# Order of two small VectorE steps in a fused attention and MLP kernel: mixing product of the outputs ahead of phi of q

**Chip, cores, metric.** One Trainium2 chip, one of its cores. The metric is the device time of one execution in microseconds (us), lower is better. Executions of a kernel agree within about 0.3%, apart from a slow state of the chip that is left aside.

## The reference, cut to what matters

The kernel computes x + A(norm(x)) + B(norm(x)). B is a token-mixing MLP. A is an attention of 32 heads over 2048 tokens in 4 segments, with softmax inside a segment and a memory M, z of the segments before. The change touches only A:

```python
phi = lambda t: jnp.where(t > 0, t + 1.0, jnp.exp(t))
for s in range(N):                                   # 4 segments of 512 tokens
    p = softmax(einsum('bhqd,bhkd->bhqk', qs, ks) * scale + mask)
    a_dot = einsum('bhqk,bhkd->bhqd', p, vs)
    pq = phi(qs)
    a_mem = einsum('bhld,bhde->bhle', pq, M) / (einsum('bhld,bhd->bhl', pq, z)[..., None] + 1e-06)
    outs.append(g * a_mem + (1.0 - g) * a_dot)       # the mixing
    M = M + einsum('bhld,bhle->bhde', phi(ks), vs); z = z + phi(ks).sum(...)
return o @ wo
```

## The kernel before

After the MLP (up to about 388 us of the span) attention runs in 32 units: unit `u` is one group of four heads in segment `u // 8`. In the iteration of unit `u` TensorE computes the logits of `u`, the outputs of `u - 1` (`weigh`, three parts), and between them dense work in matmuls of 512 columns: the projections q, k, v of later units and the output products with `wo`. ScalarE takes the exponentials, GpSimd applies the causal mask, VectorE does the rest in small steps. The steps wait in a queue, `side`; TensorE's dense work stops at fixed places, and at each stop one step is issued:

```python
N_GRP = 8; N_UNIT = 32

def dense(self, n, side=True):                      # ... cut
    stop = min(at + n, 8)
    if self.side and side:
        stop = min([stop] + [x for x in stops if x > at])
    with fw.group(reads=reads(), writes=[self.R_bank[b]]):
        for i in range(at, stop):
            mm(b, i)
    # ...
    if stop == 8:
        end(b)                                       # copy out of PSUM: qT, kT, vA or fin
        self.jobs.popleft()
    elif self.side and stop in stops:
        self.side.popleft()()                        # one small step

# attention(), iteration of unit u, after the three parts of weigh(u - 1):
if u:
    self.weigh(u - 1, 2)
    steps = self.combine(u - 1)                      # [scales, products, add]
    last = steps[-1]
    steps[-1] = lambda u=u, last=last: (last(), self.o_transpose_dma(u - 1))
    self.side.append(steps.pop(0))                   # scales
if N_GRP <= u:
    self.side.append(lambda u=u: self.phi_q(u))
if u:
    self.side.extend(steps)                          # products, add + transposing transfer
if u + 1 < N_UNIT:
    self.side.append(lambda u=u: (self.phi_k(u + 1), self.k_transpose(u + 1)))
```

The steps themselves, with the tile names that the profile shows:

```python
def phi(self, dst, R_dst, src, R_src, k, u):         # two VectorE instructions
    # ...
    mt[:] = min(et[:], 1.0)                          # "mtmp<-etmp"
    dst = max(src + 1.0, mt[:])                      # "pqT<-qT,mtmp" for q

def combine(self, u):                                # ... cut
    # scales:   two small instructions, "srec<-ost", "srec<-srec,gate"
    # products: 1024 elements a partition, "prod<-ost,srec" (srec broadcast over 32)
    # add:      512 elements a partition, "o_s<-prod"

# logits(): after the exponential of ScalarE, one GpSimd instruction a block
for v, kb, _ in blocks:
    d = self.pT[:, v % 2, :, PT_OFF[kb]:PT_OFF[kb] + P]
    fw.op("pool", lambda e: e.affine_select(d, d, pattern=[[0, 4], [1, P]], compare_op=ALU.is_ge,
                                            fill=0.0, base=0, channel_multiplier=-1), ...)

# weigh(u, part): one group of matmuls; the whole group waits for what any of it reads
reads = list(R_vA)
if s:
    reads += [self.R_pqT[k], self.R_MZbf[g]]         # phi of q of this unit, the memory
reads += [R[pb][kb] for kb in range(last + 1) for R in (self.R_pu, self.R_pd)]
```

So phi of q of unit `u` must be done when `weigh(u, 0)` begins, early in the next iteration.

## Time and profile before

| | |
|---|---|
| time, median (fast runs) | 652.8 us (652.59 to 652.9) |
| span of the profiled run | 651.1 us |
| TensorE busy | 645.8 us (99%) |
| VectorE busy | 428.1 us (66%), in 800 instructions |
| GpSimd busy | 153.9 us (24%); 128 masks take 105.3 of it |
| attention, from the first logits | 387.8 us to the end |

The names in the profile: PE is TensorE's matmuls, PEld its weight loads (they run ahead of the matmuls), DVE is VectorE, POOL is GpSimd, ACT is ScalarE, SPq the queue that issues transfers. A row of the timeline has start, duration, engine, line, operation, out<-in, shapes and count; in brackets the idle time of the engine ahead of it and what ended it. Nearly all matmuls stand under L199, a helper, so one goes by tiles. The rows themselves are in the prediction.

### The profile page before, as it was taken

The numbers are of one execution on the slowest core, as the hardware profiler recorded it, in microseconds if no ns is written. First come the engines' busy times: TensorE is split into PE (matmuls) and PEld (weight loads), VectorE is DVE, ScalarE is ACT, GpSimd is POOL, SyncE is SP. The second block draws the span as 40 slices with busy tenths as digits, with TensorE's granted clock in tenths as the row PEclk, the third lists the DMA queues.
The fourth block names the chain that finished last, engine by engine and source line by source line (L and its number), as shares of the span: only waits on it lengthen the run. The fifth ranks groups of instructions, "written<-read, shape, count | busy, mean of one in ns | idle before, by whom it ended". The sixth has DMA issues, their size and how long they took to land.

```text
span 651.1 us, 11170 instructions
## 1 busy us (share of the span) xinstructions
PE 645.8 (99%) x4611; PEld 303.2 (47%) x4611; DVE 428.1 (66%) x800; ACT 281.4 (43%) x305; POOL 153.9 (24%) x179
## 2 busy tenths in 40 slices
PE   8999999999999999999999999999999999999998
PEld 3444444444444444444444444444544444445544
DVE  6975675665556664744738325766787877777896
ACT  7543232232210000110101047778767778888770
POOL 2500000000011220220202203343334444554440
DMA  9804233242498967538262946988544456445325
GB/s 306 212 0 130 65 106 89 64 116 79 129 257 206 270 205 209 156 103 229 80 208 98 267 126 174 179 169 197 120 116 96 125 147 109 126 98 128 106 93 139
DMA packets 181963, 95.00 MB, mean 146 GB/s; under 512 B 100248, under 2 KB 167832, under 8 KB 181656
## 3 DMA queue, kind: packets, MB, share of 16 engines
q1 hardware_dynamic: 181768, 94.25, 56.3%
q8 instruction: 36, 0.59, 0.4%
q14 instruction: 15, 0.12, 0.1%
q10 hardware_dynamic: 144, 0.03, 0.0%
HBM read 69.23 MB, written 13.63 MB: 127 GB/s over the span
## 4 chain that ended last, share of the span: by engine, by line
PE 91%; DVE 5%; ACT 2%; DMA 2%; issue 1%; POOL 0%; DVEq 0%
PE ps_all L199 91%; ACT pT L1377 1%; DMA w2s<-in_B_w_dram 1%; DVE prod L1478 1%; DVE ln_st L587 1%; DVE sum L648 0%; DMA xin<-in_A_x_dram 0%; DVE mtmp L1243 0%; DVE h L627 0%; DVE mtmp L1241 0%; DVE fin L1320 0%; DVE ost L1431 0%; DVE kT L1275 0%; POOL ln_rs L611 0%; DVE part L689 0%
## 5 line engine op out<-in xcount | busy, mean ns | idle before, releaser
L1377 ACT ACTIVATE pT<-ps_all 128x2048 bf16<-128x2048 f32 x80 | 150.2, 1877 | 47.7 <-PE ps_all L199 47.2
L1381 POOL TENSOR_SCALAR_AFFINE_SELECT pT<-pT 128x512 bf16<-128x512 bf16 x128 | 105.3, 841 | 161.3 <-ACT pT L1377 161.3
L689 DVE TENSOR_TENSOR part<-ps_all,part 128x512 f32<-128x512 f32 x84 | 57.7, 690 | 109.1 <-PE ps_all L199 88.2
L1080 POOL TENSOR_TENSOR part<-part,stg 128x512 f32<-128x512 f32 x24 | 33.0, 1403 | 285.5 <-DVE part L689 285.5
L746 ACT ACTIVATE g<-part,b1c 128x512 f16<-128x512 f32 x36 | 26.0, 722 | 99.1 <-DVE part L689 99.1
L199 PE MATMUL ps_all<-wv,xnT 128*128 128x512 bf16 x256 | 68.6, 380 | 0.2
L199 PE MATMUL ps_all<-xnT,wq 128*128 128x512 bf16 (+1 forms) x256 | 66.4, 380 | 0.0
L199 PE MATMUL ps_all<-wo,oT 128*128 128x512 bf16 (+2 forms) x272 | 63.8, 367 | 0.1
L1431 DVE TENSOR_TENSOR ost<-ps_all,eps 128x396 bf16<-128x396 f32 (+1 forms) x72 | 37.1, 522 | 33.9 <-PE ps_all L199 33.3
L694 ACT ACTIVATE part<-ps_all 128x512 f32<-128x512 f32 x24 | 14.0, 596 | 101.6 <-PE ps_all L199 67.1
L199 PEld LDWEIGHTS ps_all<-vA,pT 128*128 128x128 bf16 x1280 | 45.7, 96 | 20.4 <-DVE ost L1431 1.7
L199 PE MATMUL ps_all<-g,w2s 128*128 128x512 f16 x224 | 51.0, 379 | 0.0
L199 PE MATMUL ps_all<-g,sum 128*128 128x512 f16 x224 | 51.0, 379 | 0.0
L199 PE MATMUL ps_all<-gT,sum 128*128 128x512 f16 x224 | 50.3, 379 | 0.2 <-DVE gT L663 0.2
L199 PE MATMUL ps_all<-vA,pT 128*128 128x33 bf16 x1280 | 48.5, 177 | 0.3 <-DVE ost L1431 0.3
L199 PE MATMUL ps_all<-h,sum 128*128 128x512 f16 x192 | 45.2, 379 | 0.0
L199 PE MATMUL ps_all<-h,w1s 128*128 128x512 f16 x192 | 44.9, 379 | 0.0
L199 PE MATMUL ps_all<-hT,sum 128*128 128x512 f16 x192 | 43.6, 379 | 0.0
L199 PEld LDWEIGHTS ps_all<-wo,oT 128*128 128x128 bf16 x272 | 23.8, 98 | 24.7 <-issue 3.7
L199 PEld LDWEIGHTS ps_all<-xnT,wq 128*128 128x128 bf16 x256 | 22.6, 97 | 25.4 <-issue 5.3
L199 PEld LDWEIGHTS ps_all<-gT,sum 128*128 128x128 f16 x224 | 21.8, 98 | 26.8 <-DVE gT L663 0.6
L199 PEld LDWEIGHTS ps_all<-g,w2s 128*128 128x128 bf16 x224 | 21.9, 98 | 26.4
(118 smaller groups left out, 867.7 us busy)
## 6 DMA issues: line engine op xcount, KB each, us to landing
w2s<-in_B_w_dram SPq DMA_DIRECT2D x8, 1792.0 KB, 9.7
w1s<-in_B_w_dram SPq DMA_DIRECT2D x12, 1024.0 KB, 5.6
wq<-in_A_wq_dram SPq DMA_DIRECT2D x32, 256.0 KB, 3.2
stg<-in_A_x_dram SPq DMA_DIRECT2D x16, 256.0 KB, 2.9
xs<-in_A_x_dram SPq DMA_DIRECT2D x16, 256.0 KB, 3.3
out_dram<-stg SPq DMA_DIRECT2D x16, 256.0 KB, 3.7
wk<-in_A_wk_dram SPq DMA_DIRECT2D x16, 256.0 KB, 3.6
fin<-out_dram SPq DMA_DIRECT2D x16, 256.0 KB, 3.3
```

The costliest lines, as they stand in the source:

```text
L199: ins = self.nc.tensor.matmul(*args, **kwargs)
L587: fw.op("dve", lambda e: e.bn_stats(st[:, 6 * h:6 * h + 6], src[:, 512 * h:512 * h + 512]), reads=[self.R_xin[c]], writes=[R])
L689: self.fw.op("dve", lambda e: e.tensor_tensor(self.tmp[dst][:], self.bank(b), self.tmp[src][:], op=ALU.add), reads=[self.R_bank[b], self.R ...
L694: self.fw.op("act", lambda e: e.activation(self.tmp[dst][:], self.bank(b), ACT.Copy), reads=[self.R_bank[b]], writes=[self.R_tmp[dst]])
L746: self.fw.op("act", lambda e: e.activation(self.gB[f % 2][half][:, f // 2, :], src, ACT.Gelu_apprx_tanh, bias=self.b1c[:, f:f + 1], scale= ...
L1080: fw.op("pool", lambda e: e.tensor_tensor(self.tmp[t][:], self.tmp[t][:], self.stg[k][:, 512 * half:512 * half + 512], op=ALU.add), reads= ...
L1377: fw.op("act", lambda e: e.activation(dst, src, ACT.Exp, scale=SCALE), reads=self.R_bank[0:4], writes=[R[v % 2][kb] for v, kb, _ in blocks ...
L1381: fw.op("pool", lambda e: e.affine_select(d, d, pattern=[[0, 4], [1, P]], compare_op=ALU.is_ge, fill=0.0, base=0, channel_multiplier=-1), ...
L1431: fw.op("dve", lambda e: e.tensor_tensor(dst, src, eps, op=ALU.add), reads=[self.R_bank[b], self.R_eps], writes=[self.R_ost[o][part]])
L1478: fw.op("dve", lambda e: e.tensor_tensor(self.prod[:], ost[:, :, 0:D_HEAD], rec.unsqueeze(2).to_broadcast([P, 32, D_HEAD]), op=ALU.mult), ...
```

## The change

The intent is to issue the product of the mixing one step earlier, ahead of phi of q. Unit 8 keeps the old order (the outputs of unit 7, in the first segment, have no memory part).

```diff
@@ attention()
                 self.side.append(steps.pop(0))
+            if u > N_GRP:
+                self.side.append(steps.pop(0))
             if N_GRP <= u:
                 self.side.append(lambda u=u: self.phi_q(u))
             if u:
```

## The prediction

> **What bounds the kernel now.** I read the page first, then the chain of work that ended last, then the waits of TensorE's weight loads over the stretch that the change touches, and last the timeline of single units of attention (a unit is one group of four heads in one of four segments, 32 in all, numbered 0 to 31). The page and its chain:
>
> ```profile
> PE 645.8 (99%) x4611; PEld 303.2 (47%) x4611; DVE 428.1 (66%) x800; ACT 281.4 (43%) x305; POOL 153.9 (24%) x179
> PE 91%; DVE 5%; ACT 2%; DMA 2%; issue 1%; POOL 0%; DVEq 0%
> ```
>
> TensorE carries 91% of the chain, VectorE 5%. The change touches units 9 to 31, from about 457 us on. There TensorE's weight loads waited for:
>
> ```profile
> PEld ps_all L199 <- DVE ost L1431: 1.7, 3, 0.7
> PEld ps_all L199 <- DVE kT L1275: 0.8, 2, 0.4
> PEld ps_all L199 <- DVE fin L1320: 0.8, 2, 0.4
> PEld ps_all L199 <- DVE pqT L1243: 0.5, 2, 0.2
> ```
>
> The reader sees how little is to be won. All waits for VectorE sum to 3.8 us, and part of each lies under matmuls still streaming: I took each matmul's start, less the start before it plus 0.213 us (the spacing of 512-column matmuls in this trace), and found real gaps of 0.31 us at 474.1, 0.32 at 484.5, 0.32 at 503.7, and 0.05 to 0.15 at six other places, 1.5 us in all. So TensorE is nearly gapless: a gain can't pass 1.5 us (0.2%), while a loss has no such ceiling.
>
> Now unit 15, the tightest:
>
> ```profile
> 514.78 0.19 DVE L1475 TENSOR_TENSOR srec<-srec,gate 128x32 f32<-128x32 f32 x1
> 514.89 0.68 DVE L1320 TENSOR_TENSOR fin<-ps_all,fin 128x512 bf16<-128x512 f32 x1
> 515.49 0.28 DVE L1241 TENSOR_SCALAR mtmp<-etmp 128x512 bf16<-128x512 bf16 x1
> 515.81 0.69 DVE L1243 SCALAR_TENSOR_TENSOR pqT<-qT,mtmp 128x512 bf16<-128x512 bf16 x1
> 516.02 2.54 POOL L1381 TENSOR_SCALAR_AFFINE_SELECT pT<-pT 128x512 bf16<-128x512 bf16 x2 [2.99 <-ACT pT L1377]
> 516.42 1.65 DVE L1478 TENSOR_TENSOR prod<-ost,srec 128x1024 bf16<-128x1024 bf16 x1
> 517.22 0.36 PEld L199 LDWEIGHTS ps_all<-vA,pT 128*128 128x128 bf16 x4
> 518.10 0.74 DVE L1484 TENSOR_TENSOR o_s<-prod 128x512 bf16<-128x512 bf16 x1
> ```
>
> VectorE runs without a pause. pqT (phi of q) is done at 515.81 + 0.69 = 516.50; the group of matmuls that needs it begins at 517.22. Its slack is 0.72 us. The same difference, read for every unit: 1.14 us for unit 17, 1.74 to 1.88 for the odd units 9, 19, 21, 23, 25, 27 and 29, 2.0 or more elsewhere. And unit 14:
>
> ```profile
> 506.34 0.69 DVE L1243 SCALAR_TENSOR_TENSOR pqT<-qT,mtmp 128x512 bf16<-128x512 bf16 x1
> 506.95 1.22 DVE L1478 TENSOR_TENSOR prod<-ost,srec 128x1024 bf16<-128x1024 bf16 x1
> 508.08 0.68 DVE L1320 TENSOR_TENSOR fin<-ps_all,fin 128x512 bf16<-128x512 f32 x1
> 508.82 0.11 PEld L199 LDWEIGHTS ps_all<-wv,xnT 128*128 128x128 f16 x2 [0.38 <-DVE fin L1320]
> ```
>
> Here a projection waits for fin, the copy that empties its PSUM bank, which stands in VectorE's queue behind both phi and product (unit 16 looks the same at 524.45).
>
> **What the Trainium skill says.** "GPSIMD Engine Reference", section Key points: GpSimd shares its SBUF interfaces with VectorE and contends with instructions in a 2-port mode or with two SBUF inputs. The trace agrees strongly:
>
> ```profile
> L1478 DVE TENSOR_TENSOR prod<-ost,srec x24: 1216/1218/1654, 461.4 to 639.7; 128x1024 bf16<-128x1024 bf16 x24
> L1484 DVE TENSOR_TENSOR o_s<-prod x24: 419/735/839, 466.7 to 641.0; 128x512 bf16<-128x512 bf16 x24
> L1381 POOL TENSOR_SCALAR_AFFINE_SELECT pT<-pT x128: 628/634/1722, 390.2 to 635.1; 128x512 bf16<-128x512 bf16 x128
> ```
>
> The causal mask (POOL) takes 0.63 us alone and 1.72 against the product; the product takes 1.22 or 1.65, the sum 0.42 or 0.74, mtmp 0.28 or 0.77. One side waits until the other's instruction is nearly over: in unit 15 the first mask ends at 516.99, prod ends at 518.07, which is 1.22 after 516.85, so the interface came free about 0.14 before the mask's end. fin, which reads PSUM, kept its 0.68 beside a running mask. "VectorE: DVE Perf Modes", section The perf-mode tier table, has a bf16 tensor_tensor of 2048 elements at 1224 ns in 2x mode; the 1024-element product takes 1218 ns, so with its broadcast operand it runs at half that rate and holds the interface longest. "Trainium Kernel Development and Optimization", section Performance Expectations, calls matmul busy time a bad measure; hence the gaps above rather than the 99%.
>
> **The change part by part.** Nothing is removed or added. In each of 23 units the order scales, phi (mtmp 0.28, pqT 0.69), product (1.22), sum becomes scales, product, phi, sum. The number of small steps is the same, so TensorE's order, cut at these steps, stays as it is. VectorE's work is the same, and so is the count of back-to-back dependences (product behind scales, pqT behind mtmp, instead of pqT behind mtmp, sum behind product). Three things move.
>
> (a) The product's result comes earlier, but the sum stays the fourth step, so the transposing transfer starts where it did. Worth 0.
>
> (b) pqT comes later by the product, 1.22 less the 0.08 by which independent instructions overlap: 1.14 us; and more where the two masks of the unit now fall between product and pqT. For unit 15: product 515.49 to 516.71. The mask asked at 516.02 gets the interface at about 516.57 and gives it up near 517.06; mtmp 517.06 to 517.35; second mask until about 517.70; pqT to 518.39. TensorE wanted it at 517.22, so it loses 1.15, or 0.45 without the masks. Unit 17 in the same way (product from 531.12, first mask asked at 531.66): pqT at 534.02 against 533.28, loss 0.8, or 0.1. Units 9, 19, 21, 23: pqT about 2.0 later against 1.74 of slack: 0.3 each, 1.2 in all, or nothing. In units 25, 27, 29 the mask is asked after the product's end and only one comes between: 1.7 against 1.81 to 1.88, no loss.
>
> (c) fin in units 14 and 16 stays third in line, but both masks now hold up mtmp and pqT ahead of it, where before one ran while fin used PSUM. Unit 14: product 506.14 to 507.35, mask to about 507.70, mtmp to 507.99, mask to 508.34, pqT to 509.03, fin to 509.64 instead of 508.77. Loss 0.85 each, 1.7 for both.
>
> Gain: unit 10's kT some 0.1 earlier at 474.1. Sum: 1.15 + 0.8 + 1.2 + 1.7 - 0.1 = 4.75 us if every mask falls as I lay it; 0.45 + 0.1 = 0.55 if none gets between. TensorE has no gaps to absorb it, so it adds to the end.
>
> **The rivals.**
> 1. Nothing moves: the slacks of 1.7 us and more swallow the delay, units 15 and 17 lose a few tenths. For it: the same work on VectorE, and TensorE's order unchanged. Against it: slack of 0.72 in unit 15. 653.4.
> 2. The product slips out of the mask's way, VectorE's crowded stretches (units 11, 13, 15, 17, where prod took 1.65) end earlier by up to 0.43, and the waits for ost (0.32 us gaps at 484.5 and 503.7) shrink. For it: in these units VectorE is on the chain right up to ost. Against it: the masks then hold mtmp and pqT instead; my replay of unit 11 ends the sum at 482.41 against 482.42 before. 651.6.
> 3. My own: masks between product and pqT, 4.75 us. Against it: each hand-over is a matter of 0.05 us in units 9 and 19 to 23.
> 4. Delays feed on each other (masks late, next unit's queue late): 660 or more. Against it: ScalarE and GpSimd are idle over half the time in these stretches, and VectorE catches up in each even unit.
>
> **Range and chances.** I weigh the third at about three quarters: 652.9 + 3.5 = 656.4. The low end leaves room for rival 1 and nearly all of rival 2, 651.8; the high end is the full sum and 1.6 more, 659.2. Two per cent is 13 us, out of reach of a gain that is capped at 1.5 us and nearly three times my full loss: within 2% 0.97, slower 0.02, faster 0.01. One of the three runs of before, 736.96, is a slow-state run and is left aside.
>
> **What would show it.** In the changed profile, weight loads should wait for pqT in units 15 and 17 (0.4 to 1.2 us each), and for fin in units 14 and 16 (some 0.9 more); VectorE's busy time should change by little; the product should show 1.22 nearly throughout, mtmp and pqT should stretch to 0.7 and 1.0 in its place, and the masks' longest time stay above 1 us. If the waits for ost shrink and pqT shows none, rival 2 holds and the sign of mine is wrong. If pqT and fin show waits but the end does not move, TensorE had slack that my gaps miss.

## The result and the profile after

The changed kernel takes 657.4 us (median of 6 runs, 656.97 to 658.01) against 652.82 before: ratio 1.0072, 95% interval 1.0058 to 1.0086. A ratio here is the mean time of one kernel's fast runs over that of the other's of the same rounds, so not quite the ratio of the medians. The change costs 0.7%, 4.6 us.

A comparison of the two instruction streams confirmed the static part: the order on TensorE and on ScalarE is the same, instruction for instruction. On VectorE only the order differs.

The page after, engines and the chain that ended last:

```profile
PE 647.1 (99%) x4611; PEld 303.3 (46%) x4611; DVE 435.7 (66%) x800; ACT 281.5 (43%) x305; POOL 138.5 (21%) x179
PE 89%; DVE 6%; ACT 2%; DMA 1%; issue 1%; SPq 0%
```

VectorE's busy time rose by 7.6 us and GpSimd's fell by 15.4, though both do the same work: busy time counts time spent waiting inside an instruction. Summed by tile, mtmp and pqT grew by 6.5 and 7.2 us, the masks lost 15.5, the sum (o_s) 4.0 and the product 1.9. So the swap moved such waits from the masks, the sum and the product to mtmp and pqT. The same lines as in the prediction (shortest, median and longest, in ns), now of the changed kernel:

```profile
L1478 DVE TENSOR_TENSOR prod<-ost,srec x24: 1215/1224/1584, 460.2 to 643.8; 128x1024 bf16<-128x1024 bf16 x24
L1484 DVE TENSOR_TENSOR o_s<-prod x24: 409/414/885, 466.6 to 645.0; 128x512 bf16<-128x512 bf16 x24
L1381 POOL TENSOR_SCALAR_AFFINE_SELECT pT<-pT x128: 628/635/1175, 389.8 to 638.3; 128x512 bf16<-128x512 bf16 x128
```

In the chain TensorE's share fell by 2% and VectorE's rose by 1%.

What the weight loads of TensorE waited for from 457 us on (total, times, longest):

```profile
PEld ps_all L199 <- DVE pqT L1243: 5.3, 7, 1.3
PEld ps_all L199 <- DVE fin L1320: 2.5, 2, 1.3
...
PEld ps_all L199 <- DVE ost L1431: 1.3, 2, 0.7
PEld ps_all L199 <- DMA oT<-o_s: 0.9, 1, 0.9
```

pqT went from 0.5 us to 5.3, fin from 0.8 to 2.5. The 0.5 of before was no wait of the group that reads pqT: it is 0.23 us at each of two loads of a projection (516.77 and 532.40), as long as the gap that the view calls "issue" in that place in other units; after the change it stands there as a wait for prod (0.5, 2, 0.2). A wait for a transposing transfer (oT) is new. The waits for ost, which would have shrunk had the product's earlier start emptied VectorE's queue, fell only by the 0.4 of unit 15, where TensorE now comes later itself.

Unit 15 after, VectorE's timeline and then the weight load that reads pqT:

```profile
515.56 0.68 DVE L1320 TENSOR_TENSOR fin<-ps_all,fin 128x512 bf16<-128x512 f32 x1
516.16 1.22 DVE L1478 TENSOR_TENSOR prod<-ost,srec 128x1024 bf16<-128x1024 bf16 x1
517.29 0.72 DVE L1241 TENSOR_SCALAR mtmp<-etmp 128x512 bf16<-128x512 bf16 x1
518.05 1.00 DVE L1243 SCALAR_TENSOR_TENSOR pqT<-qT,mtmp 128x512 bf16<-128x512 bf16 x1
518.97 0.41 DVE L1484 TENSOR_TENSOR o_s<-prod 128x512 bf16<-128x512 bf16 x1
```

```profile
519.11 0.17 PEld L199 LDWEIGHTS ps_all<-vA,pT 128*128 128x128 bf16 x4 [1.34 <-DVE pqT L1243]
```

```profile
516.70 1.81 POOL L1381 TENSOR_SCALAR_AFFINE_SELECT pT<-pT 128x512 bf16<-128x512 bf16 x2 [2.99 <-ACT pT L1377]
```

The product is back at its bare 1.22. mtmp takes 0.72 instead of 0.28 and pqT 1.00 instead of 0.69, because a mask ran ahead of each (GpSimd's row has both masks merged; singly they run from 516.70 to 517.87 and from 517.83 to 518.51). The weight load follows pqT's end by 0.06. From the end of the product to the end of pqT it is 1.68 us; the prediction had laid out 516.71 to 518.39, which is 1.68.

Unit 14 after, where a projection waits for the copy fin:

```profile
505.94 1.23 DVE L1478 TENSOR_TENSOR prod<-ost,srec 128x1024 bf16<-128x1024 bf16 x1
507.08 0.72 DVE L1241 TENSOR_SCALAR mtmp<-etmp 128x512 bf16<-128x512 bf16 x1
507.83 1.00 DVE L1243 SCALAR_TENSOR_TENSOR pqT<-qT,mtmp 128x512 bf16<-128x512 bf16 x1
508.76 0.68 DVE L1320 TENSOR_TENSOR fin<-ps_all,fin 128x512 bf16<-128x512 f32 x1
509.49 0.76 PEld L199 LDWEIGHTS ps_all<-wv,xnT 128*128 128x128 f16 x5 [1.25 <-DVE fin L1320]
```

fin starts 3.05 us after the scales' last instruction (505.71) instead of 2.17 before (505.91 to 508.08). Nothing was put ahead of it that wasn't there; the masks were let in ahead of mtmp and pqT.

A wait of a weight load overstates the loss, since weights are loaded while matmuls still stream. So the table gives the real gaps of TensorE in us, taken as in the prediction (start of a matmul, less the start before it plus 0.213):

| place | before | after | difference | predicted |
|---|---|---|---|---|
| unit 9, reads pqT | 0.04 | 0.32 | +0.28 | +0.3 |
| unit 10, kT | 0.31 | 0.18 | -0.13 | -0.1 |
| units 11, 13, ost | 0.32, 0.32 | 0.32, 0.33 | 0 | 0 |
| unit 14, fin | 0.05 | 0.92 | +0.87 | +0.85 |
| unit 15, pqT (before also ost, 0.09) | 0.09 | 1.01 | +0.92 | +1.15 |
| unit 16, fin | 0.05 | 0.93 | +0.88 | +0.85 |
| unit 17, pqT | 0 | 0.58 | +0.58 | +0.8 |
| units 19, 21, 23, pqT | 0.15, 0.09, 0.15 | 0.44, 0.37, 0.44 | +0.86 | +0.9 |
| tail, transposed outputs of unit 30 | 0 | 0.62 | +0.62 | none |
| sum | | | +4.88 | +4.75 |

The spans differ by 4.64, 0.24 less than this sum. The first logits of this profile came 0.37 earlier (387.39 instead of 387.76), ahead of all that was changed, and some 0.1 lies in gaps too small for the table.

### The profile page after: what moved, and what is told of

Its sections match the earlier page's. It is cut to its first block, busy times and chain, and to the rows that moved or that the text cites. A ratio compares the mean times of both kernels' runs of the same rounds, so it can differ in the third digit from the quotient of the medians.

```text
span 655.7 us, 11150 instructions
## 1 busy us (share of the span) xinstructions
PE 647.1 (99%) x4611; PEld 303.3 (46%) x4611; DVE 435.7 (66%) x800; ACT 281.5 (43%) x305; POOL 138.5 (21%) x179
## 4 chain that ended last, share of the span: by engine, by line
PE 89%; DVE 6%; ACT 2%; DMA 1%; issue 1%; SPq 0%
PE ps_all L199 89%; DVE prod L1478 1%; ACT pT L1377 1%; DMA w1early<-in_B_w_dram 1%; DVE pqT L1243 1%; DVE mtmp L1241 1%; DVE ost L1431 1%; DVE fin L1320 1%; SPq L221 0%; DMA oT<-o_s 0%; DVE MZbf L1444 0%; DVE srec L1474 0%; DVE MZ L1442 0%; DVE srec L1475 0%; DVE mtmp L1243 0%
## 5 line engine op out<-in xcount | busy, mean ns | idle before, releaser
L1381 POOL TENSOR_SCALAR_AFFINE_SELECT pT<-pT 128x512 bf16<-128x512 bf16 x128 | 89.9, 719 | 180.3 <-ACT pT L1377 180.3
L199 PEld LDWEIGHTS ps_all<-g,sum 128*128 128x128 f16 x224 | 21.9, 98 | 26.4
```

What stands on the lines that cost most here:

```text
L199: ins = self.nc.tensor.matmul(*args, **kwargs)
```

## The experiments

Twelve runs in three groups, each group on one chip beside its own runs of the kernel before (652.51, 652.65 and 652.75 us). The record marks all twelve as correct, even the two without masks, so "correct" says nothing about the masks here. Several of these profiles lack single matmul records, which leaves false gaps of 0.22 us; so I read them by stretches between two marks that every trace has, the weight loads that read pqT. From unit 14 to 17 before needs 22.50 us, from 17 to 24 it needs 53.10, in every profile with masks of an order that leaves the stretch alone (to 0.02).

### Units 15 and 17 alone

```diff
-            if u > N_GRP:
+            if u in (15, 17):
```

Expected: 

> The swap in units 15 and 17 alone. Theory (the loss is made unit by unit, where phi of q falls past the start of the group of matmuls that reads it, and nothing absorbs it): the real gaps of TensorE ahead of these two groups grew by 0.92 and 0.58 us in the changed kernel, so 1.5 us over the kernel before, 654.3, with both weight-load waits on pqT in the profile. Rival (the loss is one queue of VectorE that runs late through all 23 units and needs all of them): under 0.5 us here.

Measured: 653.99 us (653.87 to 654.18) against 652.51, +1.48; ratio 1.0023 (1.0009 to 1.0037). The stretch from unit 14 to 17 took 24.02 us, +1.52, and the rest was unchanged. The waits:

```profile
PEld ps_all L199 <- DVE pqT L1243: 2.2, 2, 1.3
```

Two swapped units make their whole loss without the others. A queue that runs late through all units is not needed.

### Units 14 and 16 alone

```diff
-            if u > N_GRP:
+            if u in (14, 16):
```

Expected: 

> The swap in units 14 and 16 alone, where no group waits for phi of q, but a projection waits for the copy fin that stands behind it. Theory: 0.87 + 0.88 = 1.75 us over before, 654.6, with two waits for fin of about 1.3 us at the weight loads. Rival (only the lateness of phi of q costs; fin's waits in the full change came from lateness handed down from unit 9 on): 0 to 0.3 us.

Measured: 654.27 us (654.23 to 654.46), +1.76; ratio 1.0027 (1.0014 to 1.0039). The waits:

```profile
PEld ps_all L199 <- DVE fin L1320: 2.5, 2, 1.2
```

They are as in the full change. This is the part of the loss that has nothing to do with when phi of q is read: an instruction behind the swapped pair comes late because the pair takes longer in the new order.

### The fourteen units without a predicted loss

```diff
-            if u > N_GRP:
+            if u in (10, 11, 12, 13, 18, 20, 22, 24, 25, 26, 27, 28, 29, 30):
```

Expected: 

> The swap in the 14 units where the theory sees no loss (10 to 13, 18, 20, 22, 24 to 30). Theory: slack covers the delay, unit 10 gains 0.13: between -0.2 and +0.1 us, 652.8, although VectorE's order is changed in most units and pqT ends about 1.7 to 2.0 us later in each. Rival (each swapped unit costs a share, 4.6 us / 23 = 0.2 each): 2.8 us more. Second rival (the product out of the masks' way empties VectorE's queue sooner in 11 and 13): 0.4 us less or better.

Measured: 652.63 us (652.4 to 652.8), +0.12; ratio 1.0001 (0.9988 to 1.0014): the same. Yet VectorE's work is disturbed in full here:

```profile
L1243 DVE SCALAR_TENSOR_TENSOR pqT<-qT,mtmp x24: 691/999/1137, 451.5 to 632.6; 128x512 bf16<-128x512 bf16 x24
```

The median pqT takes 1.0 us, as in the full change (0.69 before). The longer time costs nothing where there is slack. The second rival is out too, though not by the timed runs, whose interval is 0.8 us wide on each side: the stretch from unit 9 to 14 shrank by 0.12 us, which is unit 10's kT, and in the full change the two gaps for ost stayed at 0.32 and 0.33. The product clear of the masks in units 11 and 13 brought nothing.

### Units 9, 19, 21 and 23 alone

```diff
-            if u > N_GRP:
+            if u in (9, 19, 21, 23):
```

Expected: 

> The swap in units 9, 19, 21, 23 alone: the four whose slack of 1.74 us is overrun only because two masks come between product and phi of q. Theory: 0.26 + 0.29 + 0.28 + 0.29 = 1.1 us over before, 653.9. Rival (these waits in the changed kernel were handed down from the units ahead): about 0.

Measured: 653.88 us (653.6 to 654.26), +1.37; ratio 1.002 (1.0008 to 1.0033). In the profile the stretch from unit 17 to 24 is 54.00, +0.90, and the one from 8 to 9 is 6.98 instead of 6.69, +0.29: 1.19 us. The hand-overs that the prediction called a matter of 0.05 us all fell to the masks.

### Without the masks, both orders

The loop over `affine_select` is taken out of both kernels. The kernels leave out the causal mask, so they do not compute the reference; everything else in the program is as it was.

```diff
-        for v, kb, _ in blocks:
-            d = self.pT[:, v % 2, :, PT_OFF[kb]:PT_OFF[kb] + P]
-            fw.op("pool", lambda e: e.affine_select(d, d, ...), ...)
```

Expected of the order before: 

> The kernel before without the causal masks of GpSimd (wrong result on purpose, race-free), the base for the next run. Theory: the product shows 1.22 us in every unit, the sum 0.42; the small gaps of 0.09 to 0.15 us at 548, 563, 578 that wait for a mask go, and VectorE's queue in units 11 and 13 is 0.7 us shorter, so the 0.32 us gaps for ost may go too: 0.4 to 1.2 us under before, 651.7 to 652.5.

Expected of the changed order: 

> The changed kernel without the masks (wrong result on purpose). Theory: without a mask between product and phi of q, pqT comes only 1.14 us later: only unit 15 (slack 0.72) still loses, 0.4 to 0.5 us, and fin in 14 and 16 keeps its place: 0.4 to 0.6 us over the unmasked kernel before. Rival (the order alone costs, the masks are not needed for it): the same 4.6 us over it as with masks.

Measured: 651.56 us (651.41 to 651.6) and 652.01 us (651.88 to 652.53). The swap costs 0.45 us by the medians (0.6 by the means) instead of 4.6; no interval was taken between these two. Its VectorE instructions are bare:

```profile
L1243 DVE SCALAR_TENSOR_TENSOR pqT<-qT,mtmp x24: 691/692/693, 451.5 to 632.9; 128x512 bf16<-128x512 bf16 x24
L1241 DVE TENSOR_SCALAR mtmp<-etmp x40: 281/285/295, 378.6 to 632.5; 128x512 bf16<-128x512 bf16 x40
```

The base without masks was 0.1 us better than I had expected: in its profile all gaps for ost, kT and masks are gone, and the stretches from unit 8 to 31 are 1.46 us shorter together (0.34 is lost again behind the last of them). With the swap, unit 15 lost 0.27 us, fin 0.11 more in each of units 14 and 16 (I had expected none), and 0.25 fell in the tail. The 0.11 can be read from the starts: the product stands right behind the scales on which it depends and starts 0.03 us after their end, while mtmp started 0.08 before it. So the order alone costs some tenths; about nine tenths of the loss need the masks. Taking the masks out also takes their work away and moves the base; that the loss comes from masks running between the steps is read from the rows of units 14 and 15 above.

### Unit 31 alone, twice, and all but unit 31

The gap in the tail was not predicted. Three kernels went after it: the swap in unit 31 alone (run twice), and in all units but 31, beside the changed kernel once more.

```diff
-            if u > N_GRP:
+            if u in (31,):
```

Expected: 

> The swap in unit 31 alone. In the changed kernel a product of the tail waited 0.62 us for the transposed outputs of unit 30, which the prediction had not seen: there the sum stands behind product, phi and a copy fin, and two masks now come between. Theory: 0.5 to 0.7 us over before, 653.4. Rival (the wait arose because earlier delays shifted the transfers against each other): about 0.

Expected of the second run: 

> The swap in unit 31 alone, the same kernel again. Theory 1 (the wait in the tail is fixed by the order): a gap of about 0.5 us in this profile too, and 0.4 to 0.6 us over before in the timed runs. Theory 2 (a transfer's issue, 2.06 us instead of 0.43 ahead of the transposing one, is prolonged only in some executions): no gap here or a timed difference of 0.1 to 0.2 again.

```diff
-            if u > N_GRP:
+            if N_GRP < u < 31:
```

Expected: 

> The swap in units 9 to 30, unit 31 left as before. If the tail's wait is a real part of the loss: 0.5 to 0.6 us under the changed kernel, 4.0 over before. If it is only now and then there, as the timed runs of the swap in unit 31 alone suggest (0.12 us over before, although its profile showed a gap of 0.51): 0.1 us or less between the two. In the profile no wait for the transposed outputs either way.

And of the changed kernel again: 

> The changed kernel again, unaltered, beside the next two on one chip, to size the tail. 4.6 us over before, and in the profile the wait of about 0.6 us for the transposed outputs of unit 30 (all kernels of the earlier calls agreed to 0.01 us in the stretches between two marks where they share the order).

The expectation of the first run (0.5 to 0.7 us) failed; of the second run's, the second theory fits the times. Measured: unit 31 alone 652.77 us against 652.65 and 652.91 against 652.75, +0.12 and +0.16, ratios 1.0001 and 1.0002 with intervals on both sides of 1. The changed kernel again 657.41 us (ratio 1.0072, 1.0059 to 1.0085); all but unit 31 656.93 us (1.0065, 1.0052 to 1.0077), 0.48 less. The gap ahead of the product that reads unit 30's transposed outputs was 0.62 in the changed kernel's first profile, 0.27 in its second, 0.51 and none in those of unit 31 alone, none in all but 31.

What comes between is in the transfer queue. With unit 31 in the old order (all but 31), and in the new (unit 31 alone, second run):

```profile
639.76 0.43 SPq L221 DMA_DIRECT2D fin<-out_dram  x1
640.24 1.23 SPq L221 DMA_TRANSPOSE oT<-o_s  x1
641.51 1.80 SPq L221 DMA_DIRECT2D fin<-out_dram  x2
```

```profile
636.20 1.50 SPq L221 DMA_DIRECT2D fin<-out_dram  x1
637.74 1.19 SPq L221 DMA_TRANSPOSE oT<-o_s  x1
638.98 1.05 SPq L221 DMA_DIRECT2D fin<-out_dram  x2
```

The transposing issue is the second row; in both it starts within 0.05 us of the end of the issue ahead of it. That issue, of a load, takes 0.43 us in the old order and 2.08, 1.75, 2.06 and 1.50 in the four profiles with unit 31 swapped. The load itself is also issued 0.87 us later, measured from unit 31's first load that reads pqT: a store ahead of it waits for a copy fin, which stands behind the swapped pair. Together the transposing issue starts 1.9 to 2.5 us later. With the old order an issue is prolonged too, but another one: in all but 31 the pair behind the transposing one (1.80 instead of 1.05), in the profile of the fourteen units the transposing one itself (2.22 instead of 1.19). Without masks none is prolonged in the tail in either order, but others are (a load at 613.91 takes 1.57 us in the old order, one at 614.45 1.61 in the new), so masks are not needed for it. The gap of 0.25 in the tail without masks has no prolonged issue; there the transfer landed 5.0 us after its issue instead of 4.5.

The traces say more about the prolonged issues. The page of the kernel before counts 36 transfers of the kind "instruction" on queue q8. From 600 us on, the 14 profiles hold 36 issues that take over 0.3 us more than the shortest of their kind, and each of them overlaps one such transfer (read from the packed trace's records of single transfers). In the changed kernel it runs from 640.69 to 642.28 and the load's issue ends at 642.64; in the second run of unit 31 alone from 636.25 to 637.33, and the issue ends at 637.70. So a prolonged issue goes with a transfer of instructions, and the swap in unit 31 moved the load's issue into one. This is a coincidence in time, in every case: no run moved the instruction transfer by itself, and of the issues prolonged before 530 us some have none beside them. Why the timed runs show 0.5 us of it in the full change and 0.1 to 0.2 with unit 31 alone stays open.

### Two attempts at a version that beats both

The three large gaps of the kernel before come from phi of k, which stands in VectorE's queue ahead of the copies kT and ost that TensorE waits for. An empty step ahead of it lets the copies go first. The first attempt has the swap in unit 10 and the empty step in 11 and 13, the second only empty steps:

```diff
+            if u in (11, 13):               # first; and the swap "if u == 10"
+            if u in (10, 11, 13):           # second; no swap
+                self.side.append(lambda: None)
             if u + 1 < N_UNIT:
                 self.side.append(lambda u=u: (self.phi_k(u + 1), self.k_transpose(u + 1)))
```

Expected of the first: 

> An attempt to beat both: the swap in unit 10 alone (its copy kT came 0.13 us earlier there), and in units 11 and 13 an empty step ahead of phi of k, so that phi of k falls behind kT and the copies ost that TensorE waits for (gaps of 0.32 us each). Theory: 0.13 + 0.64, up to 1 us under before, 651.9 to 652.2. Rival (VectorE's step comes back in units 12 and 14, where fin then stands later): no gain or a loss of some tenths.

Expected of the second: 

> A version meant to beat both without any swap: phi of q ahead of the product everywhere as before, and an empty step ahead of phi of k in units 10, 11 and 13, so that the copies kT and ost that TensorE waits for come first. Theory: the gaps 0.31, 0.32 and 0.32 go and some 0.2 comes back in units 12 and 14: 0.6 to 0.8 us under before, a little better than the attempt with the swap in unit 10 (0.55 under). Rival: the empty step in 10 only moves the wait to the projection after it: no better than 0.5.

Measured: 652.1 us (651.87 to 652.25) against 652.65, ratio 0.999 (0.9978 to 1.0003); 652.21 us (652.11 to 652.47) against 652.75, ratio 0.9992 (0.9979 to 1.0006). All five runs of each lie below all nine of before of their group, but the intervals reach 1: a gain of half a microsecond, 0.1%, likely and not shown. In the profiles the stretch from unit 9 to 14 shrank from 47.71 us to 47.18 and 47.00. The second keeps 0.18 more there, and the timed runs don't tell the two apart; with 0.54 us the second fell short of the 0.6 to 0.8 expected. In the first, both gaps for ost are gone, but 0.16 us comes back at 492.64 (unit 12) and 0.10 at fin in unit 14, in part as its rival had it.

## Why the prediction was right

- **TensorE as the bound, with a gain capped at 1.5 us and no cap on a loss.** Right. No gap closed except 0.13 in unit 10 and 0.09 in unit 15, and each microsecond added inside attention came out at the end: the groups measured one by one (1.48 + 1.76 + 0.12 + 1.37, and 0.12 to 0.16 for unit 31) sum to 4.85 to 4.89 us, the full change to 4.6 or 4.7. They add up to within the noise of five sums; rival 4, delays that feed on each other, is out.
- **Masks between the product and pqT.** Right in kind and in size: 1.68 us from product to pqT, as laid out, mtmp 0.72 and pqT 1.00. That the masks are needed is shown by taking them away: 4.6 us became 0.45.
- **Units 15 and 17.** The place and the cause were right; the terms were 0.2 too large (1.15 for 0.92, 0.8 for 0.58). I took the loss from the start of the weight load, which runs about 0.2 ahead of its matmul (517.22 and 517.43 before); once it waits, the matmul follows it at once, and that lead comes off the loss. The prediction's own times for pqT give 1.17 (518.39 less 517.22) and 0.74 (534.02 less 533.28) rather than 1.15 and 0.8. Its spacing of 0.213 us is a little low too, most 512-column matmuls of that trace are 0.215 to 0.216 apart; in the differences between two profiles this cancels.
- **fin in units 14 and 16.** Right: 0.87 and 0.88 for 0.85.
- **Units 9, 19, 21, 23.** Right: 1.14 for 1.2.
- **Even units and 25 to 29.** Right: no loss (fourteen units together +0.12).
- **The weight of three quarters.** Needless caution: the sum as laid out, 4.75, was nearer than the 3.5 that I put on record. That it came so near is in part luck: two errors of opposite sign hid in it, 0.45 too much in units 15 and 17 and the tail's wait of up to 0.62 that I had not looked for. I had checked the step behind phi only where TensorE reads a copy, not where a transfer starts from the sum.
- **Part (a), "the transposing transfer starts where it did".** Wrong in unit 31: it started 1.9 to 2.5 us later, 0.87 of it because the transfers ahead of it waited for a later fin and the rest behind a prolonged issue, at a cost between 0 and 0.6 us.

## What to carry to other kernels

When steps on one engine change places, ask who reads each result first and by how much it is early; here 23 swapped units cost nothing except in eight places, which could be named from the slacks before, and at times in a ninth, unit 31, which was overlooked. A swap of equal work is not neutral if another engine shares an interface with this one: here a mask that came up during the product (1.22 us) ran ahead of mtmp, and the next one ahead of pqT, which made them 0.72 and 1.00 us long instead of 0.28 and 0.69. Judge the loss on a full TensorE from the starts of its matmuls, not from its busy share nor from the waits of its weight loads.

## What the Trainium skill lacked or had wrong

- "GPSIMD Engine Reference", Key points, says that the engines contend for the SBUF interfaces and in which forms, with which the rows above agree; fin, with one operand in PSUM, stayed at 0.68. That the later instruction waits for the earlier one stands elsewhere in the skill and is not lacking. What no page gives is the amounts: mtmp 0.28 to 0.72, pqT 0.69 to 1.00, a mask 0.63 to 1.72; in the profile the interface comes free about 0.14 us before the end of the instruction that holds it (unit 15: the product ends at 517.38, the mask at 517.87, which is 0.63 after 517.24); and a waiting mask gets in between two VectorE instructions even where these overlap by 0.08 us.
- "VectorE: DVE Perf Modes", The DRAIN you can't avoid, says that a next operation which isn't held starts earlier, without a number: here independent instructions start 0.08 us before the end of the one in front, dependent ones 0.03 after it.
- No page gives a prolonged issue of a transfer: one and the same load took 0.43 us to issue, or 1.50 to 2.08 where a transfer of instructions ran beside it.
